# A two-layer linear-attention and MLP kernel: another first chunk, first tiles transposed before they are scaled, weights behind the transposes

## The chip, the cores and the metric

The kernel runs on one core of one Trainium2 chip. The metric is the device time of one execution in microseconds, median of the runs. A profile is one execution taken by the hardware profiler, with the start and length of each instruction on TensorE (PE, with its weight loads as PEld), VectorE (DVE), ScalarE (ACT), GpSimd (POOL), and of the DMA issues of SyncE (SP) and the other queues.

## The reference

The same pair of blocks is applied twice, with the same weights. x is 2048 tokens by 512, bf16; 32 heads of 16; the MLP is 1792 wide.

```python
phi = lambda t: jnp.where(t > 0, t + 1, jnp.exp(t)) + 1e-6

def attn(y):                       # y = layernorm(x)
    q, k, v = heads(y @ wqkv)
    pq, pk = phi(q), phi(k)
    kv = einsum("bhsd,bhse->bhde", pk, v)
    z = einsum("bhsd->bhd", pk)
    den = einsum("bhqd,bhd->bhq", pq, z) + 1e-6
    return unheads(einsum("bhqd,bhde->bhqe", pq, kv) / den) @ wo

def mlp(y):                        # normalises y again
    return gelu(layernorm(y) @ w1 + b1) @ w2 + b2

x = x + attn(layernorm(x)); x = x + mlp(layernorm(x))     # twice
```

Both kernels compute this. kv and z are sums over all 2048 tokens, so no token's output can begin before all keys of that layer are done.

## The kernel before

The tokens are cut in 16 tiles of 128, four to a chunk; chunk c holds tiles 4c to 4c+3. x stays on the chip between layers. Names carry the layer 0 or 1 and the tile, or the chunk and a part: K0_7 is the K projection of tile 7 in the first layer.

**The first stage** makes K, Q and the sums of layer 0. For each tile `norm` (line 670) takes mean and variance (stats, aggr: 128x6 and 128x2), adds epsilon (veps), takes the reciprocal root on POOL (powA0, a POW of 128x1, line 700), and normalises on DVE (line 713) or ACT (line 708, which needs nmr from POOL first) into a buffer yb. One tile's statistics are sums by ACT instead (sum, sq). yb is turned so that the channels lie on the partitions: by four TensorE transposes and an ACT copy (PTA0, line 736, and tc, line 746) for the first six tiles, by a DMA transpose on SP's queue (TA0, line 723) for the other ten. K0 (four matmuls of 128x512, line 787) follows, then `phi` (line 753): exp on ACT, and either relu on ACT with a minimum and a sum on DVE or POOL, or, marked "max", a minimum and a maximum on DVE without the relu. G0 (`attn_g_held`, line 876) adds y times phi(K) over all tiles in four PSUM banks; these are held during the whole stage, and K, Q and the transposes share the other four. Z0 sums phi(K) per chunk on PE with 16 one-column matmuls. Then KV0 = G0 with the V weights, masked by heads (bdmask, made on POOL in two steps bdm0 and bdm1), and M0 with wo.

`attn_q` (line 799) makes Q either with channels on the partitions (128 channels by 512 tokens, one matmul group per 128 channels) or by tokens (128 tokens by 512, one group per tile). The second form is taken for chunks whose denominator is done by tokens on DVE and POOL (pz, red, den, rec, pr) and turned by DMA (TP); in layer 0 these are chunks 2 and 3, in layer 1 chunks 1 to 3. The other chunks use D matmuls, and Ln and Exp on ACT.

**The second stage** of layer 0 goes through the chunks 0, 1, 2, 3: output projection (WO0), residual (RA0), normalising and transposing for the MLP (TB0), W1 (line 1063, gelu on ACT, line 1069), W2 (line 1101) and residual (RB0), then normalising (A1) and K1, G1 and Q1 of layer 1. Layer 1 repeats this and ends in the stores. ScalarE has two tables of functions, exp with ln and gelu; each change costs a table load (line 1232).

**The order.** Each engine has a list of named operations, written out in `CONF["ORDER"]`. The program starts them strictly in this order; an operation that waits holds back all behind it on its engine. A small planner (`Scheduler.run`) goes through the lists with assumed costs to choose buffers and banks, and waits on semaphores are put in from the dependencies. `CONF["WAY"]` names the engine or form of operations that can be done in two ways.

**The loads.** x of chunk 0 comes as one tile on SP (x0) and three on ACT's queue (x1); the K weights half on SP, half on ACT (wk0, wk1); chunks 1 and 3, the Q weights and chunk 2 on ACT's queue (xc1, xc3, wq, xc2). The later weights go from POOL's queue (`late`, line 642): wv and wo after tile 5 is turned, w1 and w2 after all tiles are. In POOL's list wo stands between the normalisings of tiles 13 and 10, and w1, wv and w2 behind all of them.

Before the first data, PE runs ten warm-up matmuls on a tile of ones (line 658), nine of 512 columns and one of 128.

## Time and profile before

| | |
|---|---|
| runs | 329.36, 333.9, 330.52 us; median 330.52 |
| span of the profiled execution | 327.8 us (the page gives no other time of it) |
| DVE busy | 215.9 us (66%), 491 instructions |
| ACT busy | 199.9 us (61%), 340 instructions |
| POOL busy | 146.4 us (45%), 236 instructions |
| ACT table loads | 17, 21.8 us |
| W1 matmuls (line 1063) | 552, 101.0 us |
| W2 matmuls (line 1101) | 426, 96.9 us |
| granted TensorE clock | 9 tenths or more in each slice |

The span counts from the profiler's first instruction to its last event; a run's time also has what lies around it. Groups of instructions are named by the source line, the engine and the operation, then output and input buffers and their shapes; "x4" is the number of instructions; "idle" is the time that the engine stood before them, with what ended it. A busy time on PE counts the pipeline of each matmul, so two matmuls that follow each other overlap in it: what one costs in a stream is read from the distance of the starts.

### The profile page before, as it was taken

The page shows a single profiled execution, that of the slowest core. Times are in us where ns is not written, and L with a number is a line of the kernel's source. Part 1 is how long each engine was busy: PE and PEld are TensorE (multiplying, and loading weights), DVE is VectorE, ACT ScalarE, POOL GpSimd, SP SyncE. Part 2 cuts the span into 40 slices and gives each one's busy share as a digit, 9 for nine tenths or more (in the row PEclk, how much of TensorE's full clock was granted, in tenths as well). Part 3 has the DMA queues.
Part 4 walks back from the last instruction along what each step waited for, and adds up shares of the span by engine and source line. Part 5 has one row for each costly group of instructions (what it writes and reads, how often), then busy time and mean ns, then how long its engine had stood idle before and what let it go on. Part 6 is the DMA issues. An engine that isn't in the chain of part 4 may idle for free.

```text
span 327.8 us, 4729 instructions
## 1 busy us (share of the span) xinstructions
PE 318.6 (97%) x1687; PEld 158.3 (48%) x1718; DVE 215.9 (66%) x491; ACT 199.9 (61%) x340; POOL 146.4 (45%) x236
## 2 busy tenths in 40 slices
PE   6999999999999999999999999999999999999996
PEld 2444445576444444444444444458644444444444
DVE  4977877996867768274158999999787974100122
ACT  4897779577876166409983386879953544474200
POOL 3674836554740421528118624756673558200000
PEclk9999999999999999999999999999999999999999
DMA  7455590123112310022301110022232333100011
GB/s 280 136 67 127 157 368 9 34 46 68 32 33 50 64 33 18 16 48 48 66 9 23 35 32 0 8 43 42 41 81 66 80 66 79 51 0 2 32 48 48
DMA packets 46883, 20.37 MB, mean 62 GB/s; under 512 B 41932, under 2 KB 45388, under 8 KB 46860
## 3 DMA queue, kind: packets, MB, share of 16 engines
q1 hardware_dynamic: 44428, 12.60, 18.3%
q0 software_dynamic: 1056, 4.72, 4.2%
q10 hardware_dynamic: 1376, 2.75, 2.2%
q8 instruction: 13, 0.21, 0.3%
q14 instruction: 10, 0.08, 0.1%
HBM read 8.00 MB, written 2.10 MB: 31 GB/s over the span
## 4 chain that ended last, share of the span: by engine, by line
PE 89%; ACT 4%; DVE 2%; DMA 2%; issue 1%; POOL 1%; ACTq 0%
PE ps L1063 29%; PE ps L1101 28%; PE ps L1031 8%; PE ps L787 7%; PE ps L805 5%; PE ps L915 4%; PE ps L818 2%; PE ps L883 2%; ACT eb L757 2%; DMA t<-yb 1%; DMA t<-in_A_x_dram 1%; PE ps L1088 1%; PE ps L1007 1%; ACT yb L708 1%; PE ps L938 1%
## 5 line engine op out<-in xcount | busy, mean ns | idle before, releaser
L1069 ACT ACTIVATE gT<-ps,b1c 128x512 bf16<-128x512 f32 (+1 forms) x140 | 76.6, 605 | 58.7 <-PE ps L1063 58.6
L1063 PE MATMUL ps<-t,w 128*128 128x512 bf16 (+1 forms) x552 | 101.0, 336 | 0.6 <-ACT eb L757 0.2
L1101 PE MATMUL ps<-w,gT 128*128 128x512 bf16 x426 | 96.9, 379 | 0.4
L1063 PEld LDWEIGHTS ps<-t,w 128*128 128x128 bf16 x560 | 54.5, 98 | 44.5 <-ACT eb L757 0.7
L1101 PEld LDWEIGHTS ps<-w,gT 128*128 128x128 bf16 x434 | 42.4, 98 | 50.5 <-DVE xsb L1036 0.4
L757 ACT ACTIVATE eb<-ps 128x512 bf16<-128x512 f32 x64 | 37.7, 609 | 24.6 <-PE ps L787 21.3
L700 POOL TENSOR_TENSOR rstd<-veps,neghalf 128x1 f32<-128x1 f32 x64 | 37.2, 584 | 8.0 <-DVE veps L698 4.2
L1111 DVE TENSOR_TENSOR outb<-ps,xsb 128x512 bf16<-128x512 f32 x15 | 10.4, 690 | 41.9 <-PE ps L1101 38.4
L787 PE MATMUL ps<-wqkv,t 128*128 128x512 bf16 x127 | 31.4, 379 | 1.2 <-ACT t L746 0.7
L688 DVE BATCH_NORM_STATS2 stats<-xsb 128x6 f32<-128x512 f32 x48 | 32.2, 678 | 0.1
L1031 PE MATMUL ps<-gtb,t 128*128 128x512 bf16 x123 | 30.7, 379 | 0.3
L768 ACT ACTIVATE rb<-ps 128x512 bf16<-128x512 f32 x45 | 26.3, 612 | 7.6 <-POOL veps L698 3.5
L1048 POOL TENSOR_TENSOR xsb<-xsb,b2b 128x512 f32<-128x512 f32 x18 | 23.3, 1302 | 2.2 <-DVE yb L713 1.1
L693 POOL TENSOR_SCALAR veps<-mv 128x1 f32<-128x1 f32 x32 | 7.1, 223 | 34.6 <-DVE mv L690 32.3
L1232 ACT ACT_TABLE_LOAD x17 | 21.8, 1283 | 0.3
L1107 DVE TENSOR_TENSOR xsb<-ps,xsb 128x512 f32<-128x512 f32 x16 | 11.0, 686 | 16.4 <-PE ps L1101 16.4
L770 DVE TENSOR_SCALAR eb<-eb 128x512 bf16<-128x512 bf16 x45 | 15.7, 360 | 8.4 <-ACT eb L757 8.2
L713 DVE TENSOR_SCALAR yb<-xsb,mv,rstd 128x512 bf16<-128x512 f32 x27 | 14.3, 535 | 8.5 <-POOL rstd L700 8.5
L787 PEld LDWEIGHTS ps<-wqkv,t 128*128 128x128 bf16 x128 | 12.1, 98 | 16.0 <-ACT t L746 1.5
L805 PE MATMUL ps<-wqkv,t 128*128 128x512 bf16 x77 | 19.6, 379 | 0.1
L1031 PEld LDWEIGHTS ps<-gtb,t 128*128 128x128 bf16 x128 | 12.3, 98 | 14.5 <-ACT gT L1069 0.3
L708 ACT ACTIVATE yb<-xsb,nmr,rstd 128x512 bf16<-128x512 f32 x21 | 16.9, 815 | 3.5 <-POOL nmr L705 3.5
(98 smaller groups left out, 379.0 us busy)
## 6 DMA issues: line engine op xcount, KB each, us to landing
w<-in_B_w_dram POOLq DMA_DIRECT2D x4, 896.0 KB, 8.8
out_dram<-outb SPq DMA_DIRECT2D x15, 128.0 KB, 2.0
t<-in_A_x_dram ACTq DMA_DIRECT2D x3, 512.0 KB, 5.4
t<-yb SPq DMA_TRANSPOSE x56, 2.5
wqkv<-in_A_wqkv_dram ACTq DMA_DIRECT2D x1, 512.0 KB, 7.1
wo<-in_A_wo_dram POOLq DMA_DIRECT2D x1, 512.0 KB, 4.7
wqkv<-in_A_wqkv_dram POOLq DMA_DIRECT2D x1, 512.0 KB, 8.6
t<-in_A_x_dram ACTq DMA_DIRECT2D x1, 384.0 KB, 3.6
```

Source lines behind the costliest of these rows:

```text
L688: G.op("dve", lambda e: e.bn_stats(stats[:, s.slot, :], src()), 620, reads=src_keys, writes=[k + "s"], tiles=[s, *src_tiles], prio=prio, n ...
L700: G.op("pool", lambda e: e.tensor_tensor(rstd[:, s.slot:s.slot + 1], veps[:, s.slot:s.slot + 1], neghalf[:], op=ALU.pow), 570, reads=[k + ...
L757: G.op("act", lambda e: e.activation(eb[:, et.slot, :], bank(bt), ACT.Exp), 478, reads=[src_key], writes=[f"e{tag}"], tiles=[bt, et], prio ...
L768: G.op("act", lambda e: e.activation(rb[:, rt.slot, :], bank(bt), ACT.Relu), 478, reads=[src_key], writes=[f"r{tag}"], tiles=[bt, rt], pri ...
L787: ins = e.matmul(bank(b), lhsT=yTa(yT)[:, dt, k * P:(k + 1) * P], rhs=wqkv[:, dt, D:2 * D], start=(dt == 0), stop=(dt == DT - 1))
L805: ins = e.matmul(bank(b), lhsT=yTa(yT)[:, dt, k * P:(k + 1) * P], rhs=wqkv[:, dt, 0:D], start=(dt == 0), stop=(dt == DT - 1))
L1031: ins = e.matmul(bank(wb), lhsT=yTa(pq)[:, kt, k * P:(k + 1) * P], rhs=gtb[:, kt, :], start=(kt == 0), stop=(kt == DT - 1))
L1048: G.op("pool" if on_pool else "dve", lambda e: e.tensor_tensor(xsb[:, st, :], xsb[:, st, :], b2b[:], op=ALU.add), 1120 if on_pool else 600 ...
L1063: ins = e.matmul(bank(b, n), lhsT=w1[:, dt, ft * P:(ft + 1) * P], rhs=yTa(yT)[:, dt, k0 * P:k1 * P], start=(dt == 0), stop=(dt == DT - 1))
L1069: G.op("act", lambda e, ft=ft, b=b, k0=k0, k1=k1, n=n: e.activation(gT[:, g.slot, ft * 512 + k0 * P:ft * 512 + k1 * P], bank(b, n), ACT.Ge ...
L1101: ins = e.matmul(bank(b), lhsT=gT[:, g.slot, ft * 512 + k * P:ft * 512 + (k + 1) * P], rhs=w2[:, ft, :], start=(ft == 0), stop=(ft == FT - 1))
L1232: e.preload_act_table_set(sets[table])
```

## The change

Six things change.

1. **The first stage begins with chunk 3** (`C0=(3, 0, 1, 2)`), which comes last in the second stage. `FIRST` is tile 12 and `LAST` tile 11 of the first stage's sums. Chunk 3's Q is made by tokens, as before, but its Q0_3 groups and their phi now stand at the head of the lists; before, they stood near the end of the first stage and between the first gelus.

2. **Chunk 3's tiles are turned merely centred.** A new step `centre` subtracts the mean; the transposes, K and Q use the centred tile, and rstd is applied per token as the scale of the exp and relu in `phi`. G needs the normalised tile, so yb is scaled in place afterwards (`ysc`, three on DVE, one on ACT). All eight phi of these tiles take the relu form. Tile 13 has its sums on ACT.

```diff
-            by_act = head == "act"
+            by_act = eng(f"st{tag}") == "act"
+            centred = eng(f"cen{tag}") is not None
+            def centre(mean, op):
+                y = Tile(YB, f"y{tag}")
+                G.op("dve", lambda e: e.tensor_scalar(yb[:, y.slot, :], src(), mean(), None, op0=op), 300,
...
+            if centred:
+                def scaled():
+                    way = eng(f"cen{tag}")
+                    if way == "act":
+                        G.op("act", lambda e: e.activation(yb[:, y.slot, :], yb[:, y.slot, :], ACT.Copy, scale=rstd[:, s.slot:s.slot + 1]), 640,
...
+                return y, f"y{tag}", (s, k + "r", scaled)
...
-            G.op("act", lambda e: e.activation(eb[:, et.slot, :], bank(bt), ACT.Exp), 478, ...
+            G.op("act", lambda e: e.activation(eb[:, et.slot, :], bank(bt), ACT.Exp, scale=factor()), 478, ...
...
-            G.op("act", lambda e: e.activation(rb[:, rt.slot, :], bank(bt), ACT.Relu), 478, ...
+            G.op("act", lambda e: e.activation(rb[:, rt.slot, :], bank(bt), ACT.Relu, scale=factor()), 478, ...
```

3. **The loads of x and the Q weights** go from SP's queue; x of the first chunk comes in three pieces of one, one and two tiles. Only wk1 is left on ACT's queue, after the tile of ones is written.

```diff
-        dma("act", lambda e: e.dma_start(
-            t4[:, x0[0].slot, D:4 * D].rearrange("p (k d) -> p k d", k=3), rows(x_dram, 0)[:, 1:4, :]),
-            [("x0", k) for k in range(1, 4)], [x0[0]], prio=-119, name="x1", kb=384)
+        for k, n in ((1, 1), (2, 2)):
+            dma("sp", lambda e, k=k, n=n: e.dma_start(
+                t4[:, x0[HC].slot, k * D:(k + n) * D].rearrange("p (k d) -> p k d", k=n), rows(x_dram, HC)[:, k:k + n, :]),
+                [("x0", FIRST + k + i) for i in range(n)], [x0[HC]], prio=-119, name=f"x{k}", kb=128 * n)
...
-        load_chunk("act", 1, -98)
-        dma("act", lambda e: e.dma_start(wqkv[:, :, 0:D], wsrc[:, :, 0:D]), ["wq"], prio=-97, name="wq", kb=512)
+        load_chunk(cf["LQ"], C0[1], -98)
+        dma(cf["LQ"], lambda e: e.dma_start(wqkv[:, :, 0:D], wsrc[:, :, 0:D]), ["wq"], prio=-97, name="wq", kb=512)
```

SP's list begins x0, x1, wk0, x2, wq, xc0, xc1, xc2, TA0_0.

4. **All later weights wait for all transposes of the first stage.** POOL's list has them in one row, behind the last normalising: phik0_6, wo, w2_1, bdm1, wv, w1_1, w2_0, w1_0, phiq0_1_2, phiq0_1_1, and then the products pr0.

```diff
-                if st == 5:
-                    late("wv", "wv", wqkv[:, :, 2 * D:3 * D], wsrc[:, :, 2 * D:3 * D], -88, 512, [tr])
-                    late("wo", "wo", wo[:], A_wo.rearrange("(dt p) c -> p dt c", p=P), -87, 512, [tr])
...
+        late("wv", "wv", wqkv[:, :, 2 * D:3 * D], wsrc[:, :, 2 * D:3 * D], -88, 512, trs)
+        late("wo", "wo", wo[:], A_wo.rearrange("(dt p) c -> p dt c", p=P), -87, 512, trs)
```

5. **Warm-up:** seven matmuls of 512 columns and one of 128 (`N_WARM=7`).

6. **All five lists are settled anew**, with other assumed costs in the planner (DMA_LAT 800 for 1400, another rule for the bus and the DMA transposes), and banks: K, Q by tokens and transposes of the first stage get classes of their own on banks 4 to 7. TensorE turns five tiles of the first stage (12 to 15 and 1) and now tile 0 of TB0; DMA turns eleven. ACT's list changes its table 11 times, before 17. PE's list begins

```
warm PTA0_12 PTA0_13 K0_12 K0_13 PTA0_14 Q0_3_0 Q0_3_2 PTA0_15 K0_14 G0_12_0 Q0_3_1 K0_15 G0_13_0
G0_14_0 Q0_3_3 PTA0_1 K0_0 K0_1 G0_15_0 K0_3 G0_0_0 K0_2 Q0_0_2 Q0_0_0 G0_1_0 K0_8 Z0_3 K0_4 G0_2_0
```

and ACT's begins

```
wk1 sumA0_13 tcA0_12 tcA0_13 sqA0_13 reluk0_12 expk0_12 tcA0_14 expk0_13 reluk0_13 expq0_3_0
reluq0_3_0 tcA0_15 reluk0_14 expk0_14 reluq0_3_2 yscA0_15 reluk0_15 expk0_15 normA0_3 expq0_3_2
```

## The prediction, made before the changed kernel was run

> **What bounds the kernel now.** I read the page first (shares of busy time, the slices, the chain), then the chain in order of time, then busy time by 8 us stretches, and last the timeline of the first 30 us. The chain by engine:

> ```profile
> PE 89%; ACT 4%; DVE 2%; DMA 2%; issue 1%; POOL 1%; ACTq 0%
> ```

> TensorE carries the chain. Where it still lacks work is seen in the stretches (columns: window, its length, busy us and instruction count of each engine, granted clock, DMA share, GB/s):

> ```profile
> 0.00:8.00 8.00, 4.74 (x17) 1.82 (x18) 3.54 (x11) 3.21 (x6) 2.94 (x11) 1.00 0.77 278
> 8.00:16.00 8.00, 7.20 (x45) 3.39 (x44) 7.80 (x23) 6.91 (x14) 5.26 (x14) 1.00 0.42 141
> 16.00:24.00 8.00, 7.50 (x39) 3.36 (x38) 6.50 (x21) 7.75 (x15) 5.55 (x15) 1.00 0.49 69
> 24.00:32.00 8.00, 7.92 (x52) 3.86 (x52) 5.40 (x16) 6.23 (x11) 4.22 (x10) 1.00 0.58 122
> ```

> PE is short of work up to 24 us only; ScalarE is busy 7.75 of 8 us just there. The chain's start and end say what that early time is:

> ```profile
> 0.80 3.29 DMA t<-in_A_x_dram
> 4.11 0.71 DVE stats L688
> 5.29 0.57 POOL rstd L700
> 5.89 0.41 DVE yb L713
> ...
> 322.14 3.07 PE ps L1088 x28
> 325.23 0.42 DVE outb L1093
> ```

> Load of the first tile, statistics, reciprocal root, normalising; PE's useful work ends at 325.2.

> A ledger of PE. Four 512-column matmuls stand 0.86 us apart in the chain, so one takes 0.2157; a 256-column one 0.109 (52 in 5.68), a transposed tile 0.22, one z group 0.38, a KV step 0.22. Up to the first MLP matmul (64.55 us) PE has K 64, Q 64, G 64, output 32, D 8, M 4 and ZR 1 = 237 at 0.2157 = 51.1, six transposed tiles 1.3, four z groups 1.5, four KV steps 0.9: 54.9 us. So 9.7 us are lost by then. From there to 325.2 are 260.7 us for 1067 x 0.2157 (K, Q and G 64 each, output 96, MLP 336 + 434, D, M and ZR 9) + 252 x 0.109 + 2 of small steps = 259.6: only 1.1 lost. The change keeps all these counts (one transpose moves from the first stage to TB0_0). It can therefore win only from 10.8 us, and most of that is the wait for x. Two per cent is 6.6 us, about what a measurement of this kernel can tell from no change.

> **The first transposes.** The timeline at the start:

> ```profile
> 1.51 3.78 PE L658 MATMUL ps<-onesm 128*128 128x512 bf16 x10 [1.51 <-DVE onesm L620]
> 4.47 0.15 PEld L658 LDWEIGHTS ps<-onesm 128*128 128x128 bf16 x1 [0.28 <-issue]
> 4.86 0.10 PEld L658 LDWEIGHTS ps<-onesm 128*128 128x128 bf16 x1 [0.24 <-issue]
> 6.36 0.40 PE L736 MATMUL ps<-idp,yb 128*128 128x128 bf16 x4 [1.06 <-DVE yb L713]
> 7.44 1.04 PE L787 MATMUL ps<-wqkv,t 128*128 128x512 bf16 x4 [0.69 <-ACT t L746]
> 23.28 1.04 PE L787 MATMUL ps<-wqkv,t 128*128 128x512 bf16 x4 [0.50 <-DMA t<-yb]
> ```

> Of the 9.7 us, 6.36 lie before the first transpose and 3.3 behind it. Centring needs only the mean: it can start where veps stands now (5.05) instead of 5.89, so the transposes come 0.84 us earlier, at 5.5. Also x0 (128 KB, 3.3 us to land) no longer shares the bus with x1's 384 KB from another queue. Both land at 4.11 and 4.42; 384 KB at the 374 GB/s of the busiest stretch is 1.05 us, so x0 alone could land at 3.4; or nothing changes. First transposes: 4.8 to 5.5; I take 5.2, the middle, since x1 still follows within half a microsecond.

> The loads move from ACT's queue to SP's: eight issues of about 0.4 us keep SP until about 4.3, and its next job, the first DMA transpose, comes near 14. Bytes ahead decide: now K's weights are complete at 5.84 (1024 KB issued) and wq at 9.85 (2560 KB), which is 1536 KB in 4.0 us. In the new order wq closes 1536 KB (about 7.2, wanted near 8), chunks 0, 1 and 2 at about 8.5, 9.9 and 11.2, each ahead of its statistics. That costs nothing; were wq 1 us later, PE would stand up to 1 us.

> **Behind them.** Walked with the pitches of the rows (ACT 0.48 a tile, DVE statistics 0.60, centring 0.33) from x0 at 3.5: centring ends at 4.85, copy 5.9, K0_12 at 6.0, K0_13 6.9, tile 14's transpose 7.7, Q0_3_0 8.0, then a wait of 0.2 for its copy; tile 15's transpose 10.0, G0_12 11.1, K0_15 12.8, G0_14 14.5, tile 1's transpose 16.4. The DMA transposes must come next: tile 14's landed 2.2 us after its normalising (21.1 to 23.28), so tile 0, normalised near 14.1, is there at 16.3. By 24 PE would have 19 groups of 0.86 and five transposed tiles = 17.5 us done: 6.4 lost, against 9.3 now at 24.8.

> What the walk leaves out: the exponentials and relus of chunk 3 now scale by rstd. The trace has the same tile with and without a per-partition operand:

> ```profile
> L1069 ACT ACTIVATE gT<-ps,b1c 128x512 bf16<-128x512 f32 x84 | 53.9, 690 | 44.3 <-PE ps L1063 44.3
> L757 ACT ACTIVATE eb<-ps 128x512 bf16<-128x512 f32 x64 | 37.7, 609 | 24.6 <-PE ps L787 21.3 <-PE ps L818 1.7 <-PE ps L805 1.2
> ```

> Sixteen at 0.08 more are 1.3 us of ACT, where ACT is the tight engine; none of them can use the DVE maximum form, so each K and Q tile takes two ACT passes. The rescaling of four y tiles adds three DVE passes (0.33) and one ACT pass (0.6). Up to the first D matmul ACT has 50 tile passes at 0.48, six normalisings at 0.71 and 2.2 of sums: 30.4, against 28.1 now; PE has 35.5, against 33.1 (three Q groups more, one transpose less). The proportions stay, so the loss behind the first transpose lies between the walk's 1.6 and, with all 1.3 and a second missed transpose (0.99 at 23.28) on top, 3.9. I take 2.6. Head: 5.2 + 2.6 = 7.8 for 9.7: 1.9 us won.

> **Weights.** Six loads wait on POOL for every first-stage transpose, with the mask step bdm1, pr and phi(Q) products behind. The last, tile 9's, now goes out at 32.8; the walk puts it at 32, landing at 34 to 36. 4.72 MB at 374 GB/s are 12.6 us: all landed by 49, wv third in line by about 44; KV is wanted near 50, w1 near 62. bdm1 ends near 39 and zb wants it near 41. Behind them two phi(Q) sums of 1.17 (now one) hold two of ScalarE's four eb and rb buffers until about 45, as the one does now until 45.5; D wants their result near 50. Cost nothing; each microsecond beyond KV's time would be one lost. Taking this traffic from under the transposes may win back the 0.5 to 1.0 us of 23.28 (wo went out at 24.1, so I count none).

> **The lists.** ScalarE's table switches fall from 17 to 11 (chunk 3's Q no longer interrupts the gelus), six times 1.28 us of ACT; PE has all but 1.1 us covered there, so this buys at most that. A list settled anew can lose: bounds 0.3 to 3.5 us for the rest of the kernel (the upper is the loss that the head's lists show now behind the first transpose); I take 1.5, nearer to the row of 1.1. Sum: 1.9 - 0.4 = 1.5 us.

> **Fewer warm-ups.** Two of nine 512-column warm-ups go. Their weight loads stand 0.43 apart up to 4.47 and then 0.39, and nine at 0.427 and one of 0.107 would end after 5.4, not 5.29: the rate doubled at about 4.8, 3.3 us after the first. Seven end at 1.51 + 3.1 = 4.6, 0.2 short of that. Either the rate doubles anyway (cost 0; with nine, transposes at 4.8 would have to wait 0.5), or K0_12, K0_13 and Q0_3_0 run at half rate for another 3.3 us: 1.7 us lost, and twice that if a pause starts it over.

> [...]

> **The rivals.**
> - A, forecast: the head wins, the rest holds. 327.8 - 1.5 = 326.3 span. The median lies 2.7 above the span (lowest run 1.6, highest 6.1): 329.0. Own range 327.2 to 330.5. Chance 0.62.
> - B, slower: the matmuls start at half rate, decided where the gap between K0_12's matmuls is 0.43 rather than 0.22. 329.0 + 1.7 to 3.4 = 330.7 to 332.4. For it: 4.6 against 4.8; against: centred tiles' transposes follow closely. 0.17.
> - C, the head's gain doesn't arrive: x0 no earlier and ACT overfull with scaled passes, 3.9 lost behind 5.5, rest 1.5: 330.6 to 331. For it, ACT's 7.75 of 8. 0.14.
> - D, wv or w1 late: the weights wait for a transpose that slips past 45 us (or KV's operands stand behind them on POOL). From then a microsecond each; nine make 338. Against it, six us of slack. 0.04.
> - E: both head terms at their best with the early weights' contention gone and a clean rest, and shorter surroundings: under 323.9 would need 6.6 of 10.8 us. 0.03.

> Range: A, B, C, 326.4 to 332.4. Faster by over 2% is E, 0.03; slower 0.05 (D and a tail of B); within 2% the rest, 0.92.

> **What will show it.** First transpose at 4.8 to 5.5 without POOL's power step ahead of it; PE's loss at the first MLP matmul (start less 54.9) near 7.8; matmuls 0.216 apart from K0_12 on; no PE wait on wv or w; after it a loss near 1.5. I am wrong if scaled ACT passes cost more than 0.69 us, or if PE waits inside the later MLP stages.

## The result, and the profile after

The changed kernel takes 328.44 us in the median of 22 runs (327.75 to 332.12), the kernel before 330.47 us (22 runs on the same chip, 329.17 to 333.9). The ratio is 0.9946, 95% interval 0.9923 to 0.997: quicker by 2.0 us, within 2%. The forecast was 329.0.

The medians tell less than the list. After: a lower group of twelve runs at 327.75 to 328.49, one at 328.97, seven at 329.40 to 330.35, two at 331.6 and 332.1. Before: fourteen at 329.17 to 330.89, eight at 331.53 to 333.9. The lower groups' own medians are 328.22 and 329.91, 1.7 us apart. The granted clock does not tell the changed kernel's groups apart: its mean is 1.00 in all 22 runs (0.999 in one). The profiled execution after took 330.35 us (span 328.6), one of the upper group. Of the profiled one before only the span is known, 327.8; each run of the changed kernel takes 1.7 to 1.8 us more than its span, and with as much the profiled one before took about 329.5, in the lower group. So these two profiles, set side by side, show the changed kernel 0.8 us slower although the medians have it 2.0 us quicker. Why is the main question below.

The page after: the chain's shares, then the first four stretches and the one from 40 us (window, its length, busy us and instruction counts of PE, PEld, DVE, ACT, POOL, granted clock, DMA share, GB/s).

```profile
PE 94%; DMA 2%; DVE 1%; ACT 1%; issue 0%; SPq 0%; ACTq 0%
```

```profile
0.00:8.00 8.00, 5.79 (x20) 2.33 (x21) 3.57 (x11) 3.90 (x7) 2.78 (x11) 1.00 0.68 226
8.00:16.00 8.00, 8.00 (x37) 3.70 (x36) 6.12 (x22) 6.71 (x12) 2.85 (x10) 1.00 0.41 167
16.00:24.00 8.00, 7.97 (x41) 3.57 (x40) 7.21 (x22) 7.94 (x15) 4.89 (x12) 1.00 0.27 50
24.00:32.00 8.00, 7.29 (x49) 3.40 (x48) 7.77 (x25) 7.03 (x13) 5.76 (x15) 1.00 0.46 94
40.00:48.00 8.00, 7.38 (x64) 3.57 (x63) 7.27 (x18) 5.25 (x11) 4.48 (x6) 1.00 1.01 366
```

PE is busier in the first 24 us than before, by 1.05, 0.80 and 0.47 us. But look at the second row: 8.00 us busy with 37 matmuls, where 7.20 us held 45 before. The count alone misleads, since those missing are narrow ones (8 transposes of 128 columns start in it, 16 before). In columns, 15,360 were started, and 15,872 before. At 0.2157 us for 512, 15,360 columns take 6.5 us; the array was busy for 8.00. A busy array that takes longer over its columns is a slower one, and the granted clock, 1.00 in every row, does not say so. The chain of waits (start, length, what) names the place:

```profile
1.72 4.71 DMA wqkv<-in_A_wqkv_dram
6.52 3.57 PE ps L838 x8
...
27.20 3.32 DMA t<-yb
...
322.97 3.07 PE ps L1144 x28
326.04 0.02 issue
326.07 0.42 DVE outb L1149
```

The chain no longer starts at x, the statistics and the normalising; it starts at the first half of K's weights, which land at 6.43. Then tile 12's and 13's eight K matmuls take 3.57 us, 0.43 apart, where eight at 0.2157 with 0.17 of drain take 1.9. The timeline of TensorE (start, us, engine, line, operation, in brackets the idle time before it and what ended it):

```profile
1.51 3.27 PE L680 MATMUL ps<-onesm 128*128 128x512 bf16 x8 [1.51 <-DVE onesm L641]
4.59 1.32 PE L783 MATMUL ps<-idp,yb 128*128 128x128 bf16 x8
6.52 3.57 PE L838 MATMUL ps<-wqkv,t 128*128 128x512 bf16 x8 [0.61 <-DMA wqkv<-in_A_wqkv_dram]
9.88 0.63 PE L783 MATMUL ps<-idp,yb 128*128 128x128 bf16 x4
10.31 2.18 PE L856 MATMUL ps<-wqkv,t 128*128 128x512 bf16 x8
12.33 0.39 PE L783 MATMUL ps<-idp,yb 128*128 128x128 bf16 x4
```

A turned tile's four matmuls take 0.63 us at 9.88 and 0.39 at 12.33; the row of eight from 10.31 has 0.29 too much, so the rate doubled at 10.3 + 2 x 0.29 = 10.9. The array ran at half rate for the first 9.4 us of its work.

The ledger of the prediction: the first MLP matmul starts at 65.61, so 65.61 - 54.9 = 10.7 us are lost by then (9.7 before). 4.59 of them lie before the first transposes (6.36 before). 2.2 are the half rate: 1.67 in the eight (3.57 for 1.90), 0.24 in the four transposes behind them and 0.29 in the next row. An execution without it would have lost 8.5. PE's work ends at 326.04 with 260.43 us for 259.6 of work: 0.8 lost behind, 1.1 before.

### The profile page after: what moved, and what is told of

The parts are those of the page before. It is cut to its first block, busy times and chain, and to the rows that moved or that the text cites. A ratio compares the mean times of both kernels' runs of the same rounds, so it can differ in the third digit from the quotient of the medians.

```text
span 328.6 us, 4769 instructions
## 1 busy us (share of the span) xinstructions
PE 322.0 (98%) x1716; PEld 159.1 (48%) x1716; DVE 223.0 (68%) x507; ACT 194.4 (59%) x334; POOL 133.1 (41%) x223
## 3 DMA queue, kind: packets, MB, share of 16 engines
q0 software_dynamic: 1056, 4.72, 4.1%
## 4 chain that ended last, share of the span: by engine, by line
PE 94%; DMA 2%; DVE 1%; ACT 1%; issue 0%; SPq 0%; ACTq 0%
PE ps L1119 30%; PE ps L1157 29%; PE ps L838 9%; PE ps L1087 8%; PE ps L856 5%; PE ps L971 4%; PE ps L939 3%; PE ps L869 2%; DMA wqkv<-in_A_wqkv_dram 1%; DMA t<-yb 1%; PE ps L1144 1%; PE ps L1063 1%; PE ps L1017 1%; PE ps L994 1%; PE ps L783 0%
## 5 line engine op out<-in xcount | busy, mean ns | idle before, releaser
L808 ACT ACTIVATE eb<-ps 128x512 bf16<-128x512 f32 x56 | 32.5, 602 | 31.0 <-PE ps L838 25.6
L838 PE MATMUL ps<-wqkv,t 128*128 128x512 bf16 x128 | 33.6, 394 | 1.4 <-DMA t<-yb 0.7
L760 DVE TENSOR_SCALAR yb<-xsb,mv,rstd 128x512 bf16<-128x512 f32 x28 | 16.7, 602 | 13.6 <-POOL rstd L735 13.4
L733 POOL TENSOR_SCALAR veps<-mv 128x1 f32<-128x1 f32 x28 | 7.4, 276 | 43.7 <-DVE mv L722 43.0
L755 ACT ACTIVATE yb<-xsb,nmr,rstd 128x512 bf16<-128x512 f32 x20 | 15.7, 811 | 14.6 <-POOL nmr L752 14.6
L819 ACT ACTIVATE rb<-ps 128x512 bf16<-128x512 f32 x38 | 21.8, 601 | 0.2 <-PE ps L838 0.2
L821 DVE TENSOR_SCALAR eb<-eb 128x512 bf16<-128x512 bf16 x46 | 14.4, 325 | 10.1 <-ACT eb L808 10.0
L725 POOL TENSOR_SCALAR veps<-mv 128x1 f32<-128x1 f32 x32 | 8.8, 274 | 29.1 <-DVE mv L722 27.2
L856 PE MATMUL ps<-wqkv,t 128*128 128x512 bf16 x80 | 20.3, 383 | 0.0
L1104 POOL TENSOR_TENSOR xsb<-xsb,b2b 128x512 f32<-128x512 f32 x14 | 17.4, 1255 | 2.8 <-ACT yb L755 1.6
```

Source lines behind the costliest of these rows:

```text
L760: G.op("dve", lambda e: e.tensor_scalar(yb[:, y.slot, :], src(), stats[:, s.slot, 2:3] if by_act else mv[:, s.slot, 0:1], rstd[:, s.slot:s ...
L808: G.op("act", lambda e: e.activation(eb[:, et.slot, :], bank(bt), ACT.Exp, scale=factor()), 478, reads=[src_key, *more], writes=[f"e{tag}" ...
L819: G.op("act", lambda e: e.activation(rb[:, rt.slot, :], bank(bt), ACT.Relu, scale=factor()), 478, reads=[src_key, *more], writes=[f"r{tag} ...
L838: ins = e.matmul(bank(b), lhsT=yTa(yT)[:, dt, k * P:(k + 1) * P], rhs=wqkv[:, dt, D:2 * D], start=(dt == 0), stop=(dt == DT - 1))
L856: ins = e.matmul(bank(b), lhsT=yTa(yT)[:, dt, k * P:(k + 1) * P], rhs=wqkv[:, dt, 0:D], start=(dt == 0), stop=(dt == DT - 1))
L1104: G.op("pool" if on_pool else "dve", lambda e: e.tensor_tensor(xsb[:, st, :], xsb[:, st, :], b2b[:], op=ALU.add), 1120 if on_pool else 600 ...
```

## The experiments

Twelve runs: eleven of edited kernels and one of trials. The first is the changed kernel with one number edited. All kernels whose label begins with m_ share one further edit, so that the tiles' movement is a plain copy:

```diff
-                return e.dma_start_transpose(dst, yb[:, y.slot, :])
+                return e.dma_start(dst, yb[:, y.slot, :].rearrange("p (d s) -> p d s", d=DT))
```

and likewise for the phi(Q) tiles and b1 (b1 straight from memory): the same bytes go to the same place by the same queue, unturned, and every other instruction stays where it was. The output is then no longer the reference's. They are compared with each other only, and only within one chip: gate, m_before, m_after and m_warm9 ran on one, m_after_2, m_norm_first, m_x_on_act and m_early_wo_wv on a second, m_after_3, m_fill and m_b2_late on a third. The edits below were not tried on the kernel that turns its tiles, w11_after_b apart.

**Eleven warm-ups.**

```diff
-    C0=(3, 0, 1, 2), N_WARM=7, ZC=(0, 3), LQ='sp', N_HALF=1, ...
+    C0=(3, 0, 1, 2), N_WARM=11, ZC=(0, 3), LQ='sp', N_HALF=1, ...
```

> The changed kernel with eleven 512-column warm-ups. Theory W: the warm-ups end at 5.7 to 6.2 us, the first transposes come 1.2 to 1.6 us later than now, K0_12 at 7.0 to 7.5 instead of 6.5; no slow start is left at all, so the times stand in one group, near 328.6 to 329.0. Rival (the groups have another cause): two groups as before, both later by 0.5 to 1.0 us.

Measured: 330.37 us (12 runs, 329.41 to 331.18), before on that chip 331.15; ratio 0.9967 (0.9937 to 0.9997). One spread of 1.8 us with no gap over 0.4: one group, as theory W had it, though not within the 0.4 us that I gave it, and its median is 1.4 above the highest time that I expected (that chip's runs of the kernel before are 0.7 us up). Its timeline:

```profile
1.51 4.98 PE L680 MATMUL ps<-onesm 128*128 128x512 bf16 x12 [1.51 <-DVE onesm L641]
6.28 1.06 PE L783 MATMUL ps<-idp,yb 128*128 128x128 bf16 x8
7.61 1.90 PE L838 MATMUL ps<-wqkv,t 128*128 128x512 bf16 x8 [0.26 <-ACT t L793]
```

All eleven warm-ups run at half rate (they end at 6.3, 11 x 0.427 + 0.107 after 1.51; seven take 3.17 us in the trials below, 7 x 0.427 and 0.18 of drain), so the rate had not doubled at 4.8, as the prediction assumed from the kernel before; but K runs at full rate from its first matmul, though 1.1 us later. The span, 328.6, is that of the profiled seven-warm-up execution. By the ratios to the kernel before, 0.9967 here and 0.9946 with seven, whose intervals overlap, eleven warm-ups show no gain: what the fuller start saves, the longer start costs.

**When the rate doubles.** A kernel of trials alone:

```python
PATTERNS = {  # warm-ups; then (pause, narrow matmuls) ...; then 20 of 512
    "a7": (7, ((0, 8), (100, 0))),
    "a9": (9, ((0, 8), (100, 0))),
    "a11": (11, ((0, 8), (100, 0))),
    "b9": (9, ((560, 4), (240, 0))),
    "n7": (7, ((0, 8),)),
    "row": (0, ()),
}
```

> Measures by itself when TensorE's rate doubles after a rest (none of the reference is computed; the output is zeros). 72 trials, each after more than 10 us of rest: six patterns, 12 times each, ending in a row of 20 matmuls of 512 columns (4.5 us at 0.216 apart; each one at 0.43 apart adds 0.21). a7 is the changed kernel's start: 7 warm-ups, 9 narrow matmuls, a pause near 0.5 us, the row. a9 and a11 have 9 and 11 warm-ups, b9 is the start of the kernel before (9 warm-ups, a pause near 1 us, 4 narrow, a pause near 0.7), n7 is a7 without a pause, row is the row alone. Theory W (the rate doubles only after some 3.4 us in which the array was busy, counted in stretches whose phase is chance, and a pause spoils its stretch): row loses between 3.4/2 = 1.7 and 3.4 us, spread evenly; a7 and b9 fall in two kinds, rows that start at full rate and rows that lose 1 to 2 us, at least a quarter of the trials in each; a9 loses in fewer trials than a7, a11 in none or one; n7 loses less often than a7. Rival (busy time counts from the first matmul, wherever the stretch lies): a7, a9, a11, b9 and n7 all start their rows at full rate in every trial, and the half rate of the profiled execution was an accident.

Measured: a full-rate row takes 4.49 us, so what a row takes beyond that, doubled, says how long after its start the rate doubled. Four trials from the timeline (row; a7; a7; b9; L39 warm-ups, L44 narrow matmuls, L49 the row):

```profile
745.63 7.08 PE L49 MATMUL ps<-onesm 128*128 128x512 bf16 x20 [11.40 <-DVE flag L84]
765.32 2.98 PE L39 MATMUL ps<-onesm 128*128 128x512 bf16 x7 [12.61 <-DVE flag L84]
768.13 0.67 PE L44 MATMUL ps<-onesm 128*128 128x128 bf16 x9
769.21 4.49 PE L49 MATMUL ps<-onesm 128*128 128x512 bf16 x20 [0.41 <-DVE flag L84]
...
1018.21 3.17 PE L39 MATMUL ps<-onesm 128*128 128x512 bf16 x7 [12.94 <-DVE flag L84]
1021.17 1.17 PE L44 MATMUL ps<-onesm 128*128 128x128 bf16 x9
1022.75 5.07 PE L49 MATMUL ps<-onesm 128*128 128x512 bf16 x20 [0.41 <-DVE flag L84]
...
448.21 4.02 PE L39 MATMUL ps<-onesm 128*128 128x512 bf16 x9 [12.10 <-DVE flag L84]
452.02 0.31 PE L44 MATMUL ps<-onesm 128*128 128x128 bf16 x1
453.23 0.61 PE L44 MATMUL ps<-onesm 128*128 128x128 bf16 x4 [0.89 <-DVE flag L84]
454.40 5.94 PE L49 MATMUL ps<-onesm 128*128 128x512 bf16 x20 [0.56 <-DVE flag L84]
```

The row alone loses 1.39 to 2.92 us in its 12 trials: the rate doubles 2.8 to 5.8 us after its first matmul, with the same instructions every time. Where a doubling can be timed from the matmuls' starts (63 trials), all of them lie on one grid with a period of 3.413 us over the whole 1.5 ms, to within 0.03 us. The grid takes no notice of when the work starts. Whether it doubles at a grid point depends on the stretch of 3.413 us before it. Worked from the start of each matmul, a stretch busy 0.77 or more of its length always doubled the rate and one under 0.72 never did; between, two did and seven did not (busy without the 0.18 us of drain that the profile adds to a group: a row of 20 is listed at 4.49, 20 x 0.2157 are 4.31).

By pattern: a7 loses 0 in five trials and 0.06 to 0.59 in seven, never more: a pause of 0.41 alone spoils no stretch. a9 and a11 lose nothing in any. n7 loses in eleven, up to 1.04, since its row starts earlier: more often than a7, not less as I had expected. b9, with pauses of 0.89 and 0.56, loses 1.12 to 1.48 in five of twelve and nothing in seven. Theory W is right in kind and wrong for a7, where one pause is too little; it takes pauses of about a quarter of 3.41, 0.8 to 0.9 us, within one stretch. The rival is out: the losses are neither absent nor an accident.

Put on the profiled execution of the changed kernel: the rate doubled at 10.9, so the grid points before are 7.5 and 4.1. The stretch up to 4.1 holds 2.56 us of work (from 1.51), 0.75 of it, where the trials went both ways. The one up to 7.5 holds pauses of 0.11 and 0.61 and two drains, so work of some 0.68. The rate doubled after neither, and the next point is 10.9. Three profiles further down that start at half rate (m_after_2, m_early_wo_wv, m_b2_late) agree: worked in the same way, the stretches that did not double it were 0.39 to 0.72 busy, those at whose end it doubled 0.87 to 1.00.

**Copying base, before and after; nine warm-ups.** The second differs from the first by the change, the third from the second by `N_WARM=9`.

> The kernel before with one part left out: where a transposing DMA turned a tile, a plain DMA of the same size copies it unturned to the same place (b1 likewise), so the values differ and the order of all instructions stays. It serves as the base for the runs that edit the changed kernel in the same way. If the transposing DMAs set nothing in the times, 329 to 331.5 us, beside the kernel before; if their 2.5 us each held something up, up to 3 us less.

> The changed kernel with the same part left out (copies in place of turns). 1.5 to 2.5 us under the copying kernel before (327 to 329.5 us) if what the change wins lies in the first microseconds, as I hold; the same as the copying kernel before if it lies in how the transposing DMAs got by. Theory W: its times again fall in two groups some 1.5 us apart, and its profile shows K's first 8 matmuls either 1.7 to 1.9 us long (full rate) or near 3.6 (half).

> The changed kernel with copies in place of turns and 9 warm-ups where it has 7. Theory W: the warm-ups end near 5.4 (4.6 with 7), the first transposes start there, K's first matmul at 6.6 to 7.2, at full rate in nearly every execution; one group of times, 0.1 to 0.7 us above the quick group of the copying changed kernel and 0.8 to 1.5 below its slow group. Rival (the half rate is chance that no warm-up changes): the same two groups as with 7, both 0.5 to 0.9 later.

Measured on one chip: m_before 328.19 us (10 runs: six at 328.10 to 328.20, four at 329.10 to 329.30), m_after 326.78 (4 runs, 326.32 to 326.95), m_warm9 327.09 (9 runs, 326.58 to 327.57); before itself 330.06 there. Copying in place of turning is worth 1.9 us to the kernel before, so the transposing DMAs do set some of its time; the change still wins 1.4 us without them, just under what I expected. m_after's profile, K at 5.95 in full rate:

```profile
4.59 0.40 PE L783 MATMUL ps<-idp,yb 128*128 128x128 bf16 x4
5.25 0.40 PE L783 MATMUL ps<-idp,yb 128*128 128x128 bf16 x4 [0.26 <-DVE yb L701]
5.95 1.89 PE L838 MATMUL ps<-wqkv,t 128*128 128x512 bf16 x8 [0.30 <-DMA wqkv<-in_A_wqkv_dram]
```

Here the weights' first half took 4.2 us from issue to landing, not 4.7, and TensorE waited 0.30 us for it, not 0.61. With nine warm-ups there was one group of times in nine runs, 0.3 us above m_after's median, as theory W had it. But m_after's own four runs have one group too, so on this chip nothing shows what nine warm-ups save. Two of m_before's four upper runs have a mean granted clock of 0.995, which a start at half rate does not show (1.00 in the changed kernel's profile): something later in the kernel slowed these.

**Three parts undone, one at a time.** Tiles normalised before turning; the rest of the first chunk as one load on ScalarE's queue; wv and wo early.

```diff
-        "cenA0_12": "dve", "cenA0_13": "dve", "cenA0_14": "dve", "cenA0_15": "act", ...
```

```diff
-        for k, n in ((1, 1), (2, 2)):
-            dma("sp",
+        for k, n in ((1, 3),):
+            dma("act",
```

```diff
+                if st == 1:
+                    late("wv", "wv", wqkv[:, :, 2 * D:3 * D], wsrc[:, :, 2 * D:3 * D], -88, 512, [tr])
+                    late("wo", "wo", wo[:], A_wo.rearrange("(dt p) c -> p dt c", p=P), -87, 512, [tr])
...
-        late("wv", "wv", wqkv[:, :, 2 * D:3 * D], wsrc[:, :, 2 * D:3 * D], -88, 512, trs)
-        late("wo", "wo", wo[:], A_wo.rearrange("(dt p) c -> p dt c", p=P), -87, 512, trs)
```

(The lists follow each edit: no centring and scaling steps, and K0_12 ahead of tile 13's transposes; x1 ahead of wk1; wo and wv behind nmrA0_6.)

> The copying changed kernel once more (copies in place of turns), as the base for the three runs beside it and for its spread. Theory W, made sharper by the trials with the rest (the array doubled at the end of a stretch of 3.41 us, of free phase, in which it was busy at least 0.76 of the time): with 7 warm-ups the pauses before and after the second tile's transposes add up to 0.8 us only where K's weights land after 6.3 us; then about a third of the executions start K at half rate and lose 1.6 to 2.2 us. Where they land by 6.0, no phase fails: one group of times within 0.8 us. Rival: two groups whenever the weights land.

> The copying changed kernel, with the first chunk's tiles normalised before they are turned, as in the kernel before (no centring, no later scaling; copies in place of turns). First transposes near 5.4 in place of 4.6, K's first matmul 6.3 to 6.7. Theory L (K's weights, not the tile, set K's start): costs 0.2 to 0.7 us, of which some comes back since exp and relu of the first chunk are 0.1 us shorter each; the pause of 0.8 us behind the warm-ups makes the half-rate start more frequent, a second group 1.5 to 2 us above. Rival (the prediction's: the tile sets K's start): the 0.84 us that centring takes out come back in full or more, 0.8 to 1.2 us in all quick executions.

> The copying changed kernel with the rest of the first chunk (tiles 13 to 15) as one load of 384 KB on ScalarE's queue ahead of wk1, as in the kernel before (copies in place of turns). Theory: tile 13 comes at 4.9 to 5.6 in place of 4.2, the second half of wk some 0.5 to 1 us later, so K's first matmul at 6.5 to 7.2: 0.5 to 1.2 us slower. Rival (the 16 DMA engines are full either way, the order of issues matters little): within 0.3 us.

> The copying changed kernel with the loads of wv and wo issued by GpSimd near 15 to 20 us, among the normalisings, as in the kernel before, in place of behind all first-stage transposes (copies in place of turns). Theory (the late issues slow VectorE beside them and so make PE wait 0.4 to 0.6 us for the masked z): the wait for zb goes, 0.3 to 0.7 us quicker. Rival (the early bytes stand in the way of x, wq and the tiles' DMAs, which is why they were moved): 0.3 to 1.5 us slower, with longer PE waits for tiles between 20 and 30 us.

Measured on one chip:

| kernel | median us (runs) | the times | K's first 8 matmuls in the profile |
|---|---|---|---|
| m_after_2 | 327.77 (6) | 326.7 to 327.2 (3), 328.4 to 328.9 (3) | half rate; its time 328.37 |
| m_norm_first | 331.42 (10) | 328.5, 329.0, 330.3, 330.4, 331.4 to 331.7 (5), 333.4 | full rate; its time 328.45 |
| m_x_on_act | 328.46 (4) | 326.9, 328.3 to 328.8 (3) | full rate; its time 326.92 |
| m_early_wo_wv | 331.41 (10) | 331.0 to 333.0 | half rate; its time 332.84 |

m_after_2 shows the two groups, 1.2 us apart at least, and its profile lies in the upper one at half rate. The condition I gave for it (K's weights landing after 6.3) was too narrow: here tile 13 was late, and TensorE waited 0.58 us for that.

m_norm_first, base to base, costs 1.8 us between the lowest runs and 3.7 between the medians. Theory L, that K's weights hide the centring, falls:

```profile
5.49 0.40 PE L783 MATMUL ps<-idp,yb 128*128 128x128 bf16 x4 [0.70 <-DVE yb L760]
6.64 1.02 PE L838 MATMUL ps<-wqkv,t 128*128 128x512 bf16 x4 [0.76 <-DMA wqkv<-in_A_wqkv_dram]
7.50 0.39 PE L783 MATMUL ps<-idp,yb 128*128 128x128 bf16 x4
8.57 1.04 PE L838 MATMUL ps<-wqkv,t 128*128 128x512 bf16 x4 [0.69 <-ACT t L793]
```

K0_12 does wait for the weights here, 0.76 us, as L says; but tile 13's transposes then come at 7.50 and K0_13 waits 0.69 us for their copy. The list has a part in that: tile 13's transposes follow K0_12 at 7.50 without a wait, so its normalising was done by then and they stood behind K0_12. How much of the 1.8 us is the centring on the second tile and how much this list, no run here separates. By the estimate further down the longer pauses put most executions into the upper group; none of these was profiled, and two of the ten (330.3 and 330.4) have a mean clock of 0.995, so a drop later in the kernel.

m_x_on_act has one run in the lower group, within 0.2 us of m_after_2's median there (0.7 in the medians of 4 and 6 runs, with the two groups mixed): the rival, no matter, fits; the load order costs or wins nothing that these few runs show.

m_early_wo_wv: the wait for zb is gone as expected, yet it is 3.6 us slower in the median and 4.3 between the lowest runs, more than the rival allowed. Timeline, and the stretches against m_after_2's (second fence):

```profile
26.03 1.03 PE L939 MATMUL ps<-pkb,yb 128*128 128x512 bf16 x4
29.51 1.02 PE L838 MATMUL ps<-wqkv,t 128*128 128x512 bf16 x4 [2.45 <-DMA t<-yb]
30.37 0.54 PE L920 MATMUL ps<-onesm,pkb 128*128 128x1 bf16 x16
30.77 1.87 PE L838 MATMUL ps<-wqkv,t 128*128 128x512 bf16 x4
32.43 1.90 PE L939 MATMUL ps<-pkb,yb 128*128 128x512 bf16 x4
34.14 1.05 PE L838 MATMUL ps<-wqkv,t 128*128 128x512 bf16 x4
```

```profile
24.00:32.00 8.00, 5.55 (x38) 2.40 (x36) 5.60 (x18) 5.03 (x9) 4.46 (x12) 0.92 0.86 215
32.00:40.00 8.00, 8.00 (x34) 3.43 (x33) 5.00 (x15) 5.64 (x10) 3.37 (x6) 0.86 0.29 67
```

```profile
24.00:32.00 8.00, 8.00 (x53) 3.86 (x52) 7.76 (x26) 7.74 (x14) 5.52 (x14) 1.00 0.40 99
32.00:40.00 8.00, 8.00 (x67) 4.08 (x66) 5.09 (x17) 6.17 (x13) 5.78 (x7) 1.00 0.57 157
```

The weights' bytes (215 GB/s for 99) pass while TensorE waits 2.45 us for a tile's copy; in m_after_2 it does not wait for that tile. That alone is not all. The granted clock falls to 0.92 and 0.86: (0.08 + 0.14) x 8 = 1.76 us lost, or 3.5 us at half rate, one period of the grid. The matmuls show it: from 30.8 to 34.2 four take 1.9 us in place of 1.03, and both times lie on the grid that the start gives (the rate first doubled at 10.30; 6 and 7 periods of 3.413 later are 30.78 and 34.19). Behind the wait the array is back at half rate. 2.45 + 1.76 less the 0.39 of zb are 3.8; this execution's K also starts 0.5 us later than that of m_after_2's profile (6.83 for 6.32, behind a wait of 0.76 for tile 12), and these two, both half-rate starts, are 4.5 us apart. All ten runs show a mean clock of 0.994 or 0.995. The missing wait for zb says little: m_after_3 below has late loads and none either.

**Pauses filled; b2 late.** On a third chip.

```diff
-            "warm PTA0_12 PTA0_13 K0_12 ...
+            "warm PTA0_12 fill0 PTA0_13 fill1 K0_12 ...
...
+        for i in range(2):
+            G.op("pe", lambda e: e.matmul(bank(wu), lhsT=onesm[:, 0:P], rhs=onesm[:], start=True, stop=True), 427, reads=["onesm"],
+                 writes=[f"fill{i}"], tiles=[wu], prio=-300, name=f"fill{i}", lat=MM_DRAIN, n=1)
```

```diff
-            "... TA0_4 b2 TA0_6 TA0_7 TA0_5 TA0_10 TA0_11 TA0_9 b1 "
+            "... TA0_4 TA0_6 TA0_7 TA0_5 TA0_10 TA0_11 TA0_9 b2 b1 "
```

> The copying changed kernel (copies in place of turns) as the base for the two runs beside it, and for its share of executions with a half-rate start. Theory W, from the trials and the two runs so far: two groups 1.2 to 2 us apart where the pauses around tile 13's transposes add up to 0.8 us, none in the slow group where they don't; near 326.7 in the quick group. The profiled execution's K begins with 8 matmuls in 1.9 us or in 3.6, nothing between.

> The copying changed kernel with two more idle matmuls of 512 columns, one behind tile 12's transposes and one behind tile 13's, where TensorE would pause anyway (copies in place of turns). Theory W: no pause is left that can spoil a stretch, so K's first 8 matmuls take 1.9 to 2.3 us in every execution and the slow group is gone; the quick group gives up 0 to 0.4 us to the fillers. Median 0 to 0.4 above the base's quick group, highest time 0.8 to 1.5 below the base's slow group. Rival (half-rate starts come from elsewhere): two groups as in the base.

> The copying changed kernel with b2's load issued on the sync engine's queue behind all tiles of the first stage in place of ahead of tile 6 (copies in place of turns). Theory: b2's issue and bytes hold tile 6's transfer up, so TensorE's wait for it near 28 us (0.6 to 0.7 where it showed) goes: 0.2 to 0.7 us quicker than the base in like executions, and b2, wanted near 70 us, is still in time. Rival (the wait is the tile's own latency, or something behind takes its place): within 0.2 us.

Measured: m_after_3 327.32 us (6 runs, 326.93 to 327.79), m_fill 327.39 (6 runs: five at 326.45 to 327.46, one at 328.97), m_b2_late 327.24 (8 runs: five at 326.69 to 327.31, three at 328.64 to 328.70).

m_fill's profile is as hoped (K at 5.86, full rate, no pause over 0.16 us, span 324.7, the shortest of the profiles here), but its median is the base's, and one run at 328.97 stays unexplained. The base had no upper group to remove, so the run settles nothing.

m_b2_late: the lower groups differ by 0.16 us (327.16 against 327.32), as the rival had it. Its profile has no wait for tile 6, 1.04 us in the base's, and 0.38 us for zb instead; but it is an upper-group run, and m_after_2's profile, also half rate at the start and with b2 in its old place, has no wait for the tile (8.00 us busy from 24 to 32 above) and 0.39 for zb. So the missing wait does not show what b2's place does. The start of m_b2_late:

```profile
5.57 1.06 PE L783 MATMUL ps<-idp,yb 128*128 128x128 bf16 x8 [0.78 <-DVE stats L711]
6.87 3.27 PE L838 MATMUL ps<-wqkv,t 128*128 128x512 bf16 x8 [0.24 <-ACT t L793]
```

The first transposes came at 5.57, behind 0.78 us of pause after the warm-ups, and K's eight lost 1.38 us (3.27 for 1.89); the upper group stands 1.5 above the lower.

**All starts together.** For each kernel, the share of grid positions that would leave K's start at half rate, estimated from the pauses in its own profiled execution (narrow matmuls at their half-rate length) and 0.755 of 3.413 us, a share in the middle of the trials' mixed ones; beside it the runs in its upper group. With another share between 0.72 and 0.77 most estimates move by 0.1 at most, but at 0.77 m_after's is near 0.5, and at 0.72 no position costs m_after_2 more than 0.5 us.

| kernel | estimated share | upper group | profiled execution |
|---|---|---|---|
| changed kernel | 0.35 | 9 of 22 | half rate, upper |
| w11_after_b, m_warm9 | 0 | 0 of 12, 0 of 9 | full (m_warm9 after 0.5 us) |
| m_after | under 0.1 | 0 of 4 | full |
| m_after_2 | 0.48 | 3 of 6 | half rate, upper |
| m_x_on_act | 0.48 | 3 of 4 | full, lower |
| m_norm_first | 0.60 | 6 to 8 of 10 | full, lower |
| m_early_wo_wv | 0.6 | 4 of 10 | half rate, upper |
| m_b2_late | 0.60 | 3 of 8 | half rate, upper |
| m_after_3 | 0.48 | 0 of 6 | full |
| m_fill | 0.1 at most | 1 of 6 | full |

In every kernel with two groups the profile agrees with the group that its own time falls in. Eight lines of shares fit, as far as so few runs can; m_after_3 does not, and m_fill's one slow run lies further up than the 0.8 us that its pauses could cost. A profile gives one execution's pauses, and landing times move between executions (the first transposes, which wait for x's first tile, start at 4.59 us in the changed kernel's profile and at 5.57 in m_b2_late's; the first half of K's weights lands 4.2 us after its issue in m_after and 4.7 in the changed kernel), by as much as decides.

## Why the prediction came out right

Its time was right to 0.6 us, partly for the wrong reasons: in an execution without the half rate three terms of its sum were off, by -0.6, +1.3 and -0.7 us, and cancel. That they do is luck. The sum's 1.5 us won is what such an execution wins by the ledger (8.5 lost for 9.7 in the head, 0.8 for 1.1 behind it), and the lower groups are 1.7 apart. The last step put the median too high: the 2.7 added to the span was the distance of the median from one lower-group execution, 1.0 more than a run of the changed kernel takes beyond its own span. And the range's lower end, 326.4, stands in none of the rivals; A's own is 327.2.

**First transposes**, 4.8 to 5.5 with 5.2 taken: 4.59. x0 alone landed at 3.2, not 3.5, and nothing but the statistics, the mean and the centring stood before them. The seven warm-ups also end at 4.58; with nine the first transposes start at 5.43 (m_warm9's profile), a worth of fewer warm-ups that the prediction put at 0.5 if transposes came at 4.8 and then left out. The row's 0.84 us for leaving out the power step was the right mechanism: m_norm_first's first transposes come 0.90 later. It loses 1.8 us in all, its list included, since the second tile is later too, which the prediction did not count.

**Behind them**, 2.6 forecast: 10.7 - 4.59 = 6.1 in the profiled execution, 3.9 without the half rate, which is the upper bound given for it. This term is mis-sized. The walk let K0_12 follow the copy at 6.0 and did not set K's weights beside it, though the sentence on weights had them complete at 5.84; that was the kernel before's time. In the new order their first half is issued 0.46 us later, behind x1, and takes 0.4 us longer; they came at 6.43, and the 0.61 us are on the path. The other waits: 0.71 for tile 6, behind b2, 0.62 for zb and 0.39 before the first MLP matmul.

```profile
30.66 1.02 PE L838 MATMUL ps<-wqkv,t 128*128 128x512 bf16 x4 [0.71 <-DMA t<-yb]
45.59 0.61 PE L1063 MATMUL ps<-t,zb 128*128 128x512 bf16 x2 [0.62 <-DVE zb L1000]
```

**Scaled exponentials**, 0.08 us more each: right in kind, 0.70 for 0.60, a little over the 0.69 that I named as the limit. ScalarE's row by tile, x8 each:

```profile
L819 ACT ACTIVATE rb<-ps,rstd 128x512 bf16<-128x512 f32 x8 | 5.6, 705 | 1.2 <-PE ps L838 1.2
L808 ACT ACTIVATE eb<-ps,rstd 128x512 bf16<-128x512 f32 x8 | 5.6, 696 | 0.0
```

ScalarE is at 7.94 of 8 us from 16 to 24, and PE at 7.97 beside it: rival C did not come, though ScalarE has no slack left there.

**Weights**, "cost nothing": in time, no wait for wv, wo, w1 or w2, so rival D is out. Not quite free: between 37 and 46 us GpSimd issues six loads and a phi(Q) sum, and VectorE's passes ahead of zb stretch.

```profile
40.82 2.44 POOL L665 DMA_DIRECT2D w<-in_B_w_dram  x3
42.12 1.37 DVE L825 TENSOR_TENSOR t<-eb,rb 128x512 bf16<-128x512 bf16 x1
43.28 1.23 POOL L825 TENSOR_TENSOR t<-eb,rb 128x512 bf16<-128x512 bf16 x1
43.42 1.24 DVE L812 TENSOR_SCALAR eb<-eb 128x512 bf16<-128x512 bf16 x1
```

A sum of 0.41 us takes 1.37 and a minimum of 0.28 takes 1.24, each beside a GpSimd instruction; that this makes the wait for zb is argued, not shown. What the early place costs is far more, 3.6 us between the medians in these lists; the kernel before had its lists settled around it and need not have paid as much.

**Lists**, 1.5 lost behind the first MLP matmul: 0.8. Table loads fell to 11 as counted.

**Rival B**, matmuls at half rate: this is what the profiled execution did, by the mark given for it (0.43 apart), and by the times some 9 of 22 executions, of which only that one was profiled. Its price, 1.7 us or twice that, was 2.2 in that execution. It came in a share of the executions, where the forecast had it as a chance of 0.17 for all of them. The step that failed is "the rate doubled at about 4.8, 3.3 us after the first", read off one execution as though it were a property of the kernel; the trials have 2.7 to 6.0 after work without a pause. And it is not the two fewer warm-ups alone: seven of them without a pause (n7) never lost more than 1.04, with one pause of 0.41 (a7) no more than 0.59. It is the pauses behind them, for x, tile 13 and K's weights. The kernel before has them too (0.3 to 0.4 by the same estimate; 8 of 22 in its upper group, none of them profiled). But its upper group is not all of that kind. Of its 71 runs beside the experiments 25 lie above 331.5 us, and 15 of these have a mean granted clock of 0.989 to 0.995, as m_early_wo_wv has from its drop at 30 us; below 331.5 one of 46 has. I read this as half rate somewhere later in the kernel before; the changed kernel's 22 runs (0.999 to 1.00) and w11_after_b's 12 (1.00) show no such clock. That it is half rate, where it falls, and that the early loads are the reason, is not shown: no such run was profiled.

The ledger closes between the profile and the times: the profiled 330.35 less the 2.2 of the half rate is 328.15, near the middle of the lower group of 12 (328.22).

What stays open: how the 1.7 us divide over the six parts of the change (undone one at a time, centring and the weights' place alone cost more than the 1.4 us that the whole change wins with copies), why m_after_3 shows no upper group, whether the grid's position is even over launches, and how much each of the copying kernels' findings carries over in size to the kernel with turned tiles.

## What to carry to other kernels

A profile is one execution: before two profiles are set against each other, see which group of times each belongs to, and count columns per busy microsecond rather than trust a busy share or a granted clock (8.00 us busy at 1.00 held 6.5 us of columns here). At the start of a kernel, count the pauses within any 3.4 us against 0.8 us (the period and the share of the trials here), not the warm-ups; whether filler matmuls in the waits keep the rate, m_fill did not settle. A later load that makes TensorE wait some 2.5 us can cost another 1.8 on top, as in m_early_wo_wv. A load that is moved out of the way of short transfers can be worth more than the transfers' own time (m_early_wo_wv: 3.6 us between the medians, with 2.3 from issue to landing for the tiles' copies in its page).
